# Retention and gated FFN on one core: new order of the first loads, and an FFN that begins on 256 tokens

## The chip, the cores and the metric

The kernel runs on one core of one Trainium2 chip. The metric is the device time of one execution in microseconds (us). The time before is the median of four runs. Besides, one execution was taken by the hardware profiler; its page, its waits, its timeline and its chain are quoted below. Engines are called PE (matmul), PEld (PE's weight loads), DVE, ACT, POOL and SP. Loads from memory are issued mostly by POOL; SP issues the outputs and the transposes done by DMA.

## The reference

For each of 4 batches and 8 heads of width 64 a recurrent state is kept over 768 tokens; its output feeds an FFN with a sigmoid gate:

```python
for t in range(S):
    state = gamma * state + einsum('bhd,bhe->bhde', k[:, :, t], v[:, :, t])
    y[:, :, t] = scale * einsum('bhd,bhde->bhe', q[:, :, t], state)
x = y.transpose(0, 2, 1, 3).reshape(B * S, H * D)      # 3072 tokens of 512
out = (sigmoid(x @ w_gate) * (x @ w_val)) @ w_out      # 512 -> 1536 -> 512
```

Inputs and output are float32; gamma is a constant of each head.

## The kernel before

The recurrence is worked in chunks of 128 tokens. Six steps t = 0 to 5 each treat chunk t of all four batches, so 512 tokens, which stand in one tile `xT[t]` (128 x 4 x 512, bf16, model width on the partitions). A *pair* i = 2t + h holds batches 2h and 2h + 1 of chunk t; j = 0, 1 is the batch inside the pair. Batch b of the first step is `(i, j) = divmod(b, 2)`; the text also calls these four pieces of the first step chunks 0 to 3.

For each piece PE transposes k and q (or SP does it by DMA, `xbar`, from pair 4 on), multiplies them (`scores`, L204), DVE puts the mask or the decay on the product, PE multiplies by v (`intra`, L227; in the first step `first_y`, L303) and adds what the state gives (`inter`, L220); the state is carried on by `state` (L242) and DVE. In the first step there is no state, and the helpers are `first_transposes` (L288, copies at L289), `first_scores` (L204, DVE at L295), `first_y` (L303, copy to `xT[0]` at L306), `first_scaled` (POOL, L309) and `first_state` (L317).

The FFN of a step is `up` for 12 column groups n1 of 128 (each 4 matmuls of 512 columns with `wg` and 4 with `wv`, L331; ACT's sigmoid, L341; DVE's product into `hT`, L342), then `down` for four blocks of 128 tokens (12 matmuls each, L358; ACT copies, L362; SP stores, L363). The weights come in six slices for `wg` and `wv` (`load_gate_val(s)`, 256 columns, two column groups each, L79) and four for `wo` (L86), and stay.

The order of instructions on every engine is the order in which the program is written (`tc.manual_schedule()`). From step 1 on, a table `plan` says behind which group of FFN matmuls each piece of attention work stands: `block(old, new)` closes pair `old` (inter, intra) and opens pair `new` (scores, state). `block(5, 6)` stands near the end of step 1. PE's results go to eight PSUM buffers that are used in turn (`bank`).

What stands at the start: kf and qf (k and q of batch 0, float32) are loaded by SP and ACT; POOL writes three iotas (`tok`, `col`, `ahead`), then issues k and q of batches 1, 2, 3, v of pairs 0 and 1, and three slices of the gate and value weights. POOL's loads use eight semaphores in turn, so a load is issued only when the eighth before it has landed. DVE makes `ident`, `decay` and the rest. `keep_on(n)` is n matmuls of `ident` by itself into a bank that nobody reads. PE does transposes and scores of all four pieces, then `first_y` of all four, then `up` on all 512 tokens.

Of the kernel before, what the change touches and what calls it, by code (L numbers as in the profile page):

```python
# [8 lines left out]
F32 = mybir.dt.float32  # L9
BF16 = mybir.dt.bfloat16  # L10
AX = mybir.ActivationFunctionType
ALU = mybir.AluOpType
# [3 lines left out]
def kernel(  # L16
# [12 lines left out]
    nc = tc.nc  # L29
    B, H, S, D = q.shape  # L30
    N_TOK, D_MODEL = out.shape
    D_FF = moe_w_gate.shape[1]
    C = 128
# [6 lines left out]
    lg = [math.log(1.0 - 2.0 ** (-5.0 - h)) for h in range(H)]  # L40

    ctx.enter_context(tc.manual_schedule())
    const = ctx.enter_context(tc.tile_pool(name="const", bufs=1))
# [6 lines left out]
    vf, kn, qn, vs, kqT = {}, {}, {}, {}, {}  # L50
# [22 lines left out]
    wg = wpool.tile([128, KT, D_FF], BF16, name="wg")  # L73
    wv = wpool.tile([128, KT, D_FF], BF16, name="wv")
    wo = wpool.tile([128, NFF, D_MODEL], BF16, name="wo")

    def load_w(dst, w, s):
        cols = slice(s * 256, (s + 1) * 256)
        nc.gpsimd.dma_start(out=dst[:, :, cols], in_=w.rearrange("(kk p) n -> p kk n", p=128)[:, :, cols])  # L79

    def load_gate_val(s):
        load_w(wg, moe_w_gate, s)
        load_w(wv, moe_w_val, s)
# [7 lines left out]
    def first(dst, x, b, n, eng):  # L91
        eng.dma_start(out=dst, in_=x[b:b + n, :, 0:C, :].rearrange("b h s d -> s (b h) d"))  # L92
# [8 lines left out]
    def entry(t, j):  # L101
        return t[:, j * H:(j + 1) * H, :]
# [4 lines left out]
    tok = const.tile([128, NT], F32, name="tok")  # L107
    col = const.tile([128, C], F32, name="col")
    ahead = const.tile([128, C], F32, name="ahead")
    nc.gpsimd.iota(tok, pattern=[[C, NT]], base=0, channel_multiplier=1, allow_small_or_imprecise_dtypes=True)  # L110
    nc.gpsimd.iota(col, pattern=[[1, C]], base=0, channel_multiplier=0, allow_small_or_imprecise_dtypes=True)
    nc.gpsimd.iota(ahead, pattern=[[-1, C]], base=0, channel_multiplier=1, allow_small_or_imprecise_dtypes=True)
    for b in range(1, B):
        first(entry(kn[b // 2], b % 2), k, b, 1, nc.gpsimd)
        first(entry(qn[b // 2], b % 2), q, b, 1, nc.gpsimd)
    for i in range(2):
        first(vs[i], v, 2 * i, 2, nc.gpsimd)
    for s in range(3):
        load_gate_val(s)

    nlg = const.tile([128, 2, NP], F32, name="nlg")
    lgp = const.tile([128, NP], F32, name="lgp")
    lsc = const.tile([128, 1], F32, name="lsc")
    lsn = const.tile([128, 1], F32, name="lsn")
    ident = const.tile([128, 128], BF16, name="ident")
    causal = const.tile([128, 128], F32, name="causal")
    decay = const.tile([128, 2, NP, C], F32, name="decay")
# [4 lines left out]
    nc.vector.memset(lsc, math.log(scale))  # L134
    for h in range(H):
        nc.vector.memset(nlg[:, h % 2, h // 2:h // 2 + 1], -lg[h])
    nc.vector.tensor_scalar(ident, col, tok[:, 0:1], None, op0=ALU.is_equal)  # L137
    nc.vector.scalar_tensor_tensor(ahead, ahead, -1.0e6, ahead, op0=ALU.mult, op1=ALU.min)
    for e in range(2):
        nc.vector.tensor_tensor(decay[:, e], ahead.unsqueeze(1).to_broadcast([128, NP, C]),  # L140
                                nlg[:, e].unsqueeze(2).to_broadcast([128, NP, C]), op=ALU.mult)
        nc.scalar.activation(decay[:, e], decay[:, e], AX.Exp, bias=lsc)
    nc.vector.tensor_copy(entry(kn[0], 0), kf)
    nc.scalar.copy(entry(qn[0], 0), qf)

    def later_constants():
        for h in range(H):
            nc.vector.memset(lgp[h % 2 * D:(h % 2 + 1) * D, h // 2:h // 2 + 1], lg[h])
        nc.vector.tensor_tensor(tabs.rearrange("s (p e) t -> s p e t", e=2),
                                tok.unsqueeze(1).unsqueeze(1).to_broadcast([128, NP, 2, NT]),  # L150
                                nlg.rearrange("s e p -> s p e").unsqueeze(3).to_broadcast([128, NP, 2, NT]), op=ALU.mult)
        nc.vector.tensor_tensor(taby[:, 1], col.unsqueeze(1).to_broadcast([128, NP, C]),
                                lgp.unsqueeze(2).to_broadcast([128, NP, C]), op=ALU.mult)
        nc.scalar.activation(tabs, tabs, AX.Exp)
        nc.scalar.activation(taby[:, 0], taby[:, 1], AX.Exp, bias=lsc)
        nc.vector.tensor_scalar(causal, col, tok[:, 0:1], None, op0=ALU.is_ge)

    def extend_taby(t):
        nc.gpsimd.tensor_tensor(taby[:, t], taby[:, t - 1], gup.unsqueeze(2).to_broadcast([128, NP, C]), op=ALU.mult)
# [5 lines left out]
    def bank(shape, dt=F32):  # L165
        return pf.tile(shape, dt, tag="ff", name="ff")

    def half(e):
        return slice(e * D, (e + 1) * D)

    def heads(t, j, p):
        return t[:, j * H + 2 * p:j * H + 2 * p + 2, :].rearrange("s h d -> s (h d)")

    def new_kqT(i):
        kqT[i] = at.tile([128, 2, 2, NP, C], BF16, tag="kqT", name="kqT", bufs=2)
# [23 lines left out]
    def scores(i, j):  # L199
        t = kqT[i]  # L200
        sc[i, j] = (bank([128, NP, C]), bank([128, NP, C]))
        for p in range(NP):
            for e in range(2):
                nc.tensor.matmul(sc[i, j][e][:, p, :], t[half(e), 0, j, p, :], t[half(e), 1, j, p, :],  # L204
                                 start=True, stop=True)
# [78 lines left out]
    def first_transposes(i, j, engs):  # L284
        for which, (x, eng) in enumerate(zip((kn[i], qn[i]), engs)):
            tp = bank([128, NP, C], BF16)
            for p in range(NP):
                nc.tensor.transpose(tp[:, p, :], heads(x, j, p), ident)  # L288
            eng(kqT[i][:, which, j], tp)  # L289

    def first_scores(i, j):
        scores(i, j)
        for e, st in enumerate((stA, stB)):
            st[i, j] = at.tile([128, NP, C], BF16, tag=f"st{e}", name=f"st{e}", bufs=4)
            nc.vector.tensor_tensor(st[i, j], sc[i, j][e], decay[:, e], op=ALU.mult)  # L295

    def first_y(i, j, eng):
        if 0 not in xT:
            xT[0] = at.tile([128, NP, 512], BF16, tag="xT", name="xT")
        o = bank([128, NP, C])  # L300
        for p in range(NP):
            for e, st in enumerate((stA, stB)):
                nc.tensor.matmul(o[half(e), p, :], vs[i][:, j * H + 2 * p + e, :], st[i, j][:, p, :],  # L303
                                 start=(p == 0), stop=True, skip_group_check=True)
        c = (2 * i + j) * C
        eng(xT[0][:, :, c:c + C], o)  # L306
# [19 lines left out]
    def up_part(t, w, n1s, lo=0, hi=512):  # L326
        n = hi - lo
        u = bank([128, 512])
        for i, n1 in enumerate(n1s):
            for kk in range(KT):  # L330
                nc.tensor.matmul(u[:, i * n:(i + 1) * n], w[:, kk, n1 * 128:(n1 + 1) * 128], xT[t][:, kk, lo:hi],  # L331
                                 start=(kk == 0), stop=(kk == KT - 1))
        return u[:, :len(n1s) * n]

    def gate_times_val(t, n1s, lo, hi, ps):
        n = hi - lo
        if t not in hT:
            hT[t] = ffn.tile([128, NFF, 512], BF16, tag="hT", name="hT", bufs=2)
        gs = ffn.tile([128, 512], F32, tag="gs", name="gs")
        g = gs[:, :len(n1s) * n]  # L340
        nc.scalar.activation(g, ps[0], AX.Sigmoid)  # L341
        nc.vector.tensor_tensor(hT[t][:, n1s[0]:n1s[-1] + 1, lo:hi], g.rearrange("p (i n) -> p i n", n=n),  # L342
                                ps[1].rearrange("p (i n) -> p i n", n=n), op=ALU.mult)

    def up(t, n1s, lo=0, hi=512):
        gate_times_val(t, n1s, lo, hi, [up_part(t, w, n1s, lo, hi) for w in (wg, wv)])
# [35 lines left out]
    def keep_on(n):  # L382
        u = bank([128, 512])
        for _ in range(n):
            nc.tensor.matmul(u[:, :128], ident, ident, start=True, stop=True)  # L385
# [3 lines left out]
    act, dve = nc.scalar.copy, nc.vector.tensor_copy  # L389
    new_kqT(0)  # L390
    new_kqT(1)
    keep_on(12)
    first_transposes(0, 0, (dve, act))
    keep_on(4)
    first_scores(0, 0)
    first_transposes(0, 1, (act, act))
    later_constants()
    keep_on(4)
    first_scores(0, 1)
    first_transposes(1, 0, (act, act))  # L400
    keep_on(4)
    first_scores(1, 0)
    first_transposes(1, 1, (act, act))
    nc.scalar.preload_act_table(AX.Sigmoid)
    keep_on(4)
    first_scores(1, 1)
    keep_on(4)
    first_y(0, 0, act)
    first_y(0, 1, act)
    keep_on(8)  # L410
    first_y(1, 0, act)
    first_y(1, 1, dve)
    first_scaled(0, 0, kf)
    first_scaled(0, 1, entry(kn[0], 1))
    load_gate_val(3)
# [1 line left out]
    first_scaled(1, 1, entry(kn[1], 1))  # L417
    load_gate_val(4)
    load_gate_val(5)
    for n1 in range(4):  # L420
        up(0, (n1,))
    first_state(0)
    up(0, (4,))
    first_state(1)
    up(0, (5,))
    load_out(0)
    load_out(1)
    for p in range(NP):
# [109 lines left out]
```

## Time and profile before

| what | value |
|---|---|
| median of 4 runs | 231.98 us (231.11, 231.46, 232.51, 232.83) |
| the profiled execution's own time | 232.83 us |
| its span, first to last instruction | 231.1 us |
| PE busy | 220.8 us (96%) |
| POOL, DVE, ACT busy | 108.7, 102.5, 76.4 us |
| first FFN matmul (L331) starts | 18.58 us |
| PE's waits after 15 us | 0.88 before L331, 0.19 before L204 at 89.97, 0.95 before L242 at 92.24 |
| software DMA queue (POOL's loads) | 16.52 MB in 61,664 packets |

How to read it: a line of a timeline begins with the start in us from the span's start and the duration in us, then engine, line, operation, tiles written and read, shapes, and the number of instructions merged; in brackets stands the engine's idle time before it and what ended it. A line of waits gives the total, the number and the longest. In a line of the chain stand start, duration and what the chain ran over. Strings of digits show 40 equal slices of the span, 5.8 us each, in tenths of busy time. A DMA that appears as a POOL or SP line is its issue; its landing comes later.

### The profile page before, as it was taken

The page shows a single profiled execution, that of the slowest core. Times are in us where ns is not written, and L with a number is a line of the kernel's source. Part 1 is how long each engine was busy: PE and PEld are TensorE (multiplying, and loading weights), DVE is VectorE, ACT ScalarE, POOL GpSimd, SP SyncE. Part 2 cuts the span into 40 slices and gives each one's busy share as a digit, 9 for nine tenths or more (in the row PEclk, how much of TensorE's full clock was granted, in tenths as well). Part 3 has the DMA queues.
Part 4 walks back from the last instruction along what each step waited for, and adds up shares of the span by engine and source line. Part 5 has one row for each costly group of instructions (what it writes and reads, how often), then busy time and mean ns, then how long its engine had stood idle before and what let it go on. Part 6 is the DMA issues. An engine that isn't in the chain of part 4 may idle for free.

```text
span 231.1 us, 4377 instructions
## 1 busy us (share of the span) xinstructions
PE 220.8 (96%) x1792; PEld 120.9 (52%) x1792; DVE 102.5 (44%) x179; ACT 76.4 (33%) x127; POOL 108.7 (47%) x128
## 2 busy tenths in 40 slices
PE   4788999999999998999999999999999999999994
PEld 3673444558888654444545444545444544444444
DVE  5643543144764654733922733922634912243301
ACT  5563353336233121333222333222343212433221
POOL 8999949899999844999972100000000000000000
PEclk9999999999999999999999999999999999999999
DMA  9999999999999999999992450012410012100022
GB/s 130 149 186 197 196 190 203 226 148 266 143 191 138 154 133 202 227 142 229 206 185 91 109 120 1 3 44 93 115 23 0 3 47 93 46 1 0 0 94 91
DMA packets 84405, 27.81 MB, mean 120 GB/s; under 512 B 72097, under 2 KB 80161, under 8 KB 84385
## 3 DMA queue, kind: packets, MB, share of 16 engines
q0 software_dynamic: 61664, 16.52, 74.0%
q1 hardware_dynamic: 21536, 10.69, 21.4%
q10 hardware_dynamic: 1184, 0.33, 0.6%
q8 instruction: 14, 0.23, 0.4%
q14 instruction: 7, 0.05, 0.1%
HBM read 28.31 MB, written 6.29 MB: 150 GB/s over the span
## 4 chain that ended last, share of the span: by engine, by line
PE 59%; POOL 21%; DMA 16%; issue 2%; DVE 0%; POOLq 0%
PE ff L331 36%; PE ff L358 18%; DMA wo<-in_moe_w_out_dram 8%; DMA kn<-in_k_dram 4%; DMA qn<-in_q_dram 4%; POOL vs L196 3%; POOL kn L67 2%; POOL wg L79 2%; POOL wv L79 2%; POOL qn L67 2%; POOL ks L309 2%; POOL vf L57 2%; PE ff L227 1%; POOL kn L92 1%; PE ff L204 1%
## 5 line engine op out<-in xcount | busy, mean ns | idle before, releaser
L342 DVE TENSOR_TENSOR hT<-gs,ff 128x512 bf16<-128x512 f32 x72 | 49.2, 687 | 68.8 <-PE ff L331 62.7
L331 PE MATMUL ff<-xT,wg 128*128 128x512 bf16 (+1 forms) x336 | 74.1, 349 | 0.9 <-DVE xT L306 0.9
L331 PE MATMUL ff<-xT,wv 128*128 128x512 bf16 (+1 forms) x336 | 74.0, 349 | 0.0
L341 ACT ACTIVATE gs<-ff 128x512 f32<-128x512 f32 x72 | 43.0, 597 | 78.0 <-PE ff L331 75.8
L358 PE MATMUL ff<-wo,hT 128*128 128x512 bf16 x276 | 62.1, 379 | 0.0
L331 PEld LDWEIGHTS <-wv 128*128 128x128 bf16 x336 | 32.9, 98 | 29.4
L331 PEld LDWEIGHTS <-wg 128*128 128x128 bf16 x336 | 32.1, 98 | 29.3 <-issue 1.0
L358 PEld LDWEIGHTS <-hT 128*128 128x128 bf16 x276 | 26.3, 98 | 30.7
L362 ACT COPY ob<-ff 128x512 f32<-128x512 f32 x23 | 13.4, 585 | 53.3 <-PE ff L358 49.4
L235 DVE TENSOR_TENSOR xT<-ff,taby 128x512 bf16<-128x512 f32 x20 | 12.9, 686 | 33.2 <-PE ff L227 33.2
L210 DVE TENSOR_TENSOR st<-ff,causal 128x512 bf16<-128x512 f32 x40 | 24.8, 681 | 6.3 <-PE ff L204 6.3
L196 POOL TENSOR_TENSOR vs<-vf,tabs 128x1024 bf16<-128x1024 f32 x10 | 19.7, 1974 | 6.7 <-PE ff L227 5.8
L67 POOL DMA_DIRECT2D qn<-in_q_dram x20 | 15.3, 781 | 6.6 <-DMA qn<-in_q_dram 5.8
L67 POOL DMA_DIRECT2D kn<-in_k_dram x20 | 15.1, 763 | 0.3 <-issue 0.3
L57 POOL DMA_DIRECT2D vf<-in_v_dram x10 | 12.0, 1198 | 1.5 <-DMA wo<-in_moe_w_out_dram 1.0
L63 POOL DMA_DIRECT2D kn<-in_k_dram x10 | 9.3, 933 | 0.0
L63 POOL DMA_DIRECT2D qn<-in_q_dram x10 | 9.1, 911 | 0.4 <-DMA kn<-in_k_dram 0.4
L255 ACT CAST zb<-za 128x512 bf16<-128x512 f32 x10 | 6.1, 617 | 8.4 <-DVE za L251 8.4
L385 PE MATMUL ff<-ident 128*128 128x128 bf16 x40 | 5.4, 303 | 1.6 <-DVE ident L137 1.6
L295 DVE TENSOR_TENSOR st<-ff,decay 128x512 bf16<-128x512 f32 x8 | 5.2, 686 | 3.6 <-PE ff L204 3.6
L227 PE MATMUL ff<-st,vs 128*64 128x128 bf16 x160 | 6.4, 222 | 0.0
L204 PE MATMUL ff<-kqT 64*128 64x128 bf16 x64 | 3.7, 259 | 1.8 <-ACT kqT L289 1.8
(66 smaller groups left out, 117.6 us busy)
## 6 DMA issues: line engine op xcount, KB each, us to landing
out_dram<-ob SPq DMA_DIRECT2D x23, 256.0 KB, 2.1
vf<-in_v_dram POOLq DMA_DIRECT2D x10, 512.0 KB, 7.8
kn<-in_k_dram POOLq DMA_DIRECT2D x13, 128.0 KB, 7.2
qn<-in_q_dram POOLq DMA_DIRECT2D x13, 128.0 KB, 6.6
wg<-in_moe_w_gate_dram POOLq DMA_DIRECT2D x6, 256.0 KB, 7.9
wv<-in_moe_w_val_dram POOLq DMA_DIRECT2D x6, 256.0 KB, 8.7
wo<-in_moe_w_out_dram POOLq DMA_DIRECT2D x4, 384.0 KB, 8.6
kn<-in_k_dram POOLq DMA_DIRECT2D x20, 64.0 KB, 7.0
```

The lines of the kernel that those rows point to most:

```text
L57: nc.gpsimd.dma_start(out=vf[i], in_=v[2 * h:2 * h + 2, :, t * C:(t + 1) * C, :].rearrange("b h s d -> s (b h) d"))
L63: nc.gpsimd.dma_start(out=tiles[i][:, 0:H], in_=src[0])
L67: nc.gpsimd.dma_start(out=dst[:, e], in_=pairs[:, 1 - e])
L79: nc.gpsimd.dma_start(out=dst[:, :, cols], in_=w.rearrange("(kk p) n -> p kk n", p=128)[:, :, cols])
L196: eng.tensor_tensor(vs[i][:, j0 * H:(j0 + n) * H, :].rearrange("s (j h) d -> s j h d", j=n), vf[i][:, j0 * H:(j0 + n) * H, :].rearrange("s ...
L210: nc.vector.tensor_tensor(st[i, j], sc[i, j][e], causal4, op=ALU.mult)
L235: nc.vector.tensor_tensor(xT[t][:, :, c:c + C], y[i, j], taby[:, t], op=ALU.mult)
L331: nc.tensor.matmul(u[:, i * n:(i + 1) * n], w[:, kk, n1 * 128:(n1 + 1) * 128], xT[t][:, kk, lo:hi], start=(kk == 0), stop=(kk == KT - 1))
L341: nc.scalar.activation(g, ps[0], AX.Sigmoid)
L342: nc.vector.tensor_tensor(hT[t][:, n1s[0]:n1s[-1] + 1, lo:hi], g.rearrange("p (i n) -> p i n", n=n), ps[1].rearrange("p (i n) -> p i n", n ...
L358: nc.tensor.matmul(o, hT[t][:, n1, b * C:(b + 1) * C], wo[:, n1, :], start=(n1 == 0), stop=(n1 == NFF - 1))
L362: nc.scalar.copy(ob, o)
```

## The change

Four things are changed, all in the first 30 us of the program.

- Loads: `ahead` is the only iota before POOL's first load. Then come k and q of batch 1, v of pair 0, the other two iotas, k and q of batch 2, the first slice of the gate and value weights, v of batch 2, k and q of batch 3, v of batch 3, and the second and third slice. v of pair 1 is loaded by two issues.
- Constants: `ident` and `causal` are made from `ahead` alone; `causal` and the eight `lgp` memsets move ahead of the copy of kf; `later_constants()` is called before `first_scores(0, 0)`.
- PE's order: `first_y` of chunk 0 comes right behind the scores of chunk 1, then transposes of chunk 2, `first_y` of chunk 1 and the scores of chunk 2. FFN groups 0 and 1 are then worked on tokens 0 to 255 (N = 256), then on 256 to 383 (N = 128); groups 2 and 3 on tokens 0 to 383 (N = 384), and all four on 384 to 511 (N = 128). Chunk 3 is transposed and scored between these.
- `keep_on` counts 61 matmuls in all instead of 40, and `first_state(0)` and `first_state(1)` come one column group later.

PE's program grows from 3,586 to 3,724 instructions, 138 more.

```diff
+    nc.gpsimd.iota(ahead, pattern=[[-1, C]], base=0, channel_multiplier=1, allow_small_or_imprecise_dtypes=True)
+
+    def first_kq(b):
+        first(entry(kn[b // 2], b % 2), k, b, 1, nc.gpsimd)
+        first(entry(qn[b // 2], b % 2), q, b, 1, nc.gpsimd)
+
+    first_kq(1)
+    first(vs[0], v, 0, 2, nc.gpsimd)
     nc.gpsimd.iota(tok, pattern=[[C, NT]], base=0, channel_multiplier=1, allow_small_or_imprecise_dtypes=True)
     nc.gpsimd.iota(col, pattern=[[1, C]], base=0, channel_multiplier=0, allow_small_or_imprecise_dtypes=True)
-    nc.gpsimd.iota(ahead, pattern=[[-1, C]], base=0, channel_multiplier=1, allow_small_or_imprecise_dtypes=True)
-    for b in range(1, B):
-        first(entry(kn[b // 2], b % 2), k, b, 1, nc.gpsimd)
-        first(entry(qn[b // 2], b % 2), q, b, 1, nc.gpsimd)
-    for i in range(2):
-        first(vs[i], v, 2 * i, 2, nc.gpsimd)
-    for s in range(3):
-        load_gate_val(s)
+    first_kq(2)
+    load_gate_val(0)
+    first(entry(vs[1], 0), v, 2, 1, nc.gpsimd)
+    first_kq(3)
+    first(entry(vs[1], 1), v, 3, 1, nc.gpsimd)
+    load_gate_val(1)
+    load_gate_val(2)
...
-    nc.vector.tensor_scalar(ident, col, tok[:, 0:1], None, op0=ALU.is_equal)
+    nc.vector.tensor_scalar(ident, ahead, 0.0, None, op0=ALU.is_equal)
+    nc.vector.tensor_scalar(causal, ahead, 0.0, None, op0=ALU.is_le)
...
+    for h in range(H):
+        nc.vector.memset(lgp[h % 2 * D:(h % 2 + 1) * D, h // 2:h // 2 + 1], lg[h])
     nc.vector.tensor_copy(entry(kn[0], 0), kf)
...
     def later_constants():
-        for h in range(H):
-            nc.vector.memset(lgp[h % 2 * D:(h % 2 + 1) * D, h // 2:h // 2 + 1], lg[h])
...
-        nc.vector.tensor_scalar(causal, col, tok[:, 0:1], None, op0=ALU.is_ge)
...
-    keep_on(12)
+    keep_on(26)
     first_transposes(0, 0, (dve, act))
-    keep_on(4)
+    later_constants()
+    keep_on(5)
     first_scores(0, 0)
     first_transposes(0, 1, (act, act))
-    later_constants()
+    keep_on(8)
+    first_scores(0, 1)
+    first_y(0, 0, act)
     keep_on(4)
-    first_scores(0, 1)
-    first_transposes(1, 0, (act, act))
-    keep_on(4)
+    first_transposes(1, 0, (act, dve))
+    first_y(0, 1, act)
     first_scores(1, 0)
-    first_transposes(1, 1, (act, act))
     nc.scalar.preload_act_table(AX.Sigmoid)
     keep_on(4)
-    first_scores(1, 1)
-    keep_on(4)
-    first_y(0, 0, act)
-    first_y(0, 1, act)
-    keep_on(8)
+    up(0, (0, 1), 0, 256)
     first_y(1, 0, act)
-    first_y(1, 1, dve)
     first_scaled(0, 0, kf)
...
     load_gate_val(5)
-    for n1 in range(4):
-        up(0, (n1,))
+    keep_on(8)
+    up(0, (0, 1), 256, 384)
+    first_transposes(1, 1, (act, dve))
+    keep_on(6)
+    first_scores(1, 1)
+    ps = [up_part(0, w, (n1,), 0, 384) for w in (wg, wv) for n1 in (2, 3)]
+    gate_times_val(0, (2,), 0, 384, (ps[0], ps[2]))
+    first_y(1, 1, act)
+    gate_times_val(0, (3,), 0, 384, (ps[1], ps[3]))
+    up(0, (0, 1, 2, 3), 384, 512)
+    up(0, (4,))
     first_state(0)
-    up(0, (4,))
+    up(0, (5,))
     first_state(1)
-    up(0, (5,))
```

More of the change, by code (lines that the diff above doesn't have):

```diff
@@ L125 @@
     lsc = const.tile([128, 1], F32, name="lsc")
-    lsn = const.tile([128, 1], F32, name="lsn")
     ident = const.tile([128, 128], BF16, name="ident")
```

## The prediction

> **What bounds the kernel now.** I read the page first, then PE's timeline of the start, who PE waits for, the chain that ended last, and the timelines of SP and PE around 90 us.
>
> ```profile
> PE 220.8 (96%) x1792; PEld 120.9 (52%) x1792; DVE 102.5 (44%) x179; ACT 76.4 (33%) x127; POOL 108.7 (47%) x128
> PE   4788999999999998999999999999999999999994
> DMA  9999999999999999999992450012410012100022
> ```
>
> PE is the bound, with its holes in the first three slices (5.8 us each). But DMA is full over the first 22 slices, to 127 us: a second bound runs under the first.
>
> ```profile
> 4.65 0.61 PE L288 MATMUL ff<-ident,kn 128*128 128x128 bf16 x4 [1.62 <-DVE kn L143]
> ...
> 11.92 0.61 PE L204 MATMUL ff<-kqT 64*128 64x128 bf16 x8 [0.98 <-ACT kqT L289]
> ...
> 15.31 1.06 PE L303 MATMUL ff<-st,vs 128*64 128x128 bf16 x16
> ...
> 17.07 0.64 PE L303 MATMUL ff<-st,vs 128*64 128x128 bf16 x16
> 18.58 1.02 PE L331 MATMUL ff<-xT,wg 128*128 128x512 bf16 x4 [0.88 <-DVE xT L306]
> ```
>
> Useful FFN work begins at 18.58. The same 16 matmuls of L303 take 1.06 us at 15.31 and 0.64 at 17.07: PE runs slow until about 16.7 (128 columns go out every 107 ns) and fast after (56 ns).
>
> ```profile
> PE ff L242 <- DMA qn<-in_q_dram: 1.0, 1, 1.0
> PE ff L331 <- DVE xT L306: 0.9, 1, 0.9
> PE ff L204 <- DMA kqX<-qn: 0.2, 1, 0.2
> ```
>
> These are all of PE's waits after 15 us. Two lie at 90 us; in the timeline:
>
> ```profile
> 75.93 2.63 SPq L187 DMA_TRANSPOSE kqX<-qn  x1
> ...
> 89.97 0.62 PE L204 MATMUL ff<-kqX 64*128 64x128 bf16 x16 [0.19 <-DMA kqX<-qn]
> ...
> 90.99 0.29 PE L242 MATMUL ff<-vs,kn 128*64 128x64 bf16 x8
> 92.24 0.32 PE L242 MATMUL ff<-vs,kn 128*64 128x64 bf16 x8 [0.95 <-DMA qn<-in_q_dram]
> ```
>
> The transposed q of pair 6, issued at 75.93, lands 13.9 us later, at 89.83, and scores(6) starts at 89.97. So PE has no slack there: time won before 90 us is kept only as far as that transpose also comes sooner. The chain says the same:
>
> ```profile
> 60.25 1.96 POOL vs L196
> ...
> 72.99 10.13 DMA kn<-in_k_dram
> 83.12 0.30 issue
> 83.42 8.69 DMA qn<-in_q_dram
> ```
>
> From the start to 92 us it is POOL and DMA throughout, never PE.
>
> **The change, part by part.** Times below are from the span's start.
>
> *Loads.* POOL's first load now follows one iota (0.23) instead of three: 1.12 instead of 1.42, -0.30. The tok and col iotas (0.35 together) come behind the third load, and v of pair 1 goes in two issues (2 x 0.88 against 1.19), so POOL reaches the ks products 0.6 late (14.1 for 13.51). That is hidden by the backlog: loads issued there land 8 us later, and from 29.37 POOL itself waits for earlier loads to land (29.37, 30.70, 32.67, 34.61 in its timeline), so DMA sets its pace again. Without that cover the 0.6 would pass on to every later load. Landings of before come 0.85 to 0.9 apart for 256 KB of k or q, 1.7 for 512 KB of v, 1.3 to 1.4 for a weight slice. Stacked in the new order from 5.55: v of chunks 0 and 1 lands at 8.8 (12.5 before), k2/q2 at 9.7/10.5, slice 0 at 11.9 and 13.2 (15.5, 16.9), v2 14.1, k3/q3 14.9/15.8 (9.4, 10.2), slice 1 at 18.0 and 19.3 (18.2, 19.9), slice 2 by 22.0 (22.4). The whole DMA stream is thus 0.3 to 0.5 earlier; I take 0.4 and keep 0 and 0.6.
>
> *Constants.* ident, causal, ahead, both decays and the eight lgp memsets take 0.29 + 0.28 + 0.28 + 1.29 + 0.76 of DVE from 1.12: done at about 4.05, and kf lands at 4.14. Cover left: 0.1 us; anything over delays the first transpose by as much. In later_constants DVE's 0.90 goes into its 1.59 idle before L295, ACT's 0.96 into its 1.24 before the next kqT copy. Nothing on the path.
>
> *PE's start.* keep_on has 61 matmuls instead of 40; they fill waits. Up to scores(0,1) (9.0) nothing moves, because kf, qf and the copies set the pace. Then, at the slow clock: y of chunk 0 0.86, four idle matmuls 0.43, transposes of chunk 2 0.86, y of chunk 1 0.86, scores 0.54, four more 0.43: 13.5. xT of two chunks is written at 13.4, slice 0 is there. At the fast clock: 16 x 110 ns to 15.3; y of chunk 2 and eight idle to 16.2; wait for its xT to 16.5; 16 x 56 ns to 17.4; transposes of chunk 3, six idle, wait for the kqT copy, scores to 18.8; the 384-column groups 16 x 163 ns to 21.4 (their wv lands 19.3, wanted at 20.1; behind that wait stand y(1,1) and all of FFN); y 0.45; wait for xT 0.8 (the old 0.88 again); 32 x 56 ns to 24.5. There four column groups are done, as at 25.5 before: PE leads by 1.0. If the fast clock comes at 10 instead of 13.4 the same sum gives 23.7, a lead of 1.8; if it comes at 16.8 as before, 26.2: 0.7 behind. PE now has no hole over 0.15 us from 6.7 to 13.5, against 0.31, 0.98 and 0.31 before, and its speed-up at 16.7 came after 2.5 us with none; so 1.0 to 1.8, about 1.4.
>
> [...]
>
> *The 90 us point.* PE comes to scores(6) 1.4 early and waits for a transpose that is 0.4 early: 1.0 of the lead is lost, 0.4 stays. PE's outputs of block 0 (SP, from 49 us) also go out 1.4 sooner; they only change places with loads.
>
> *The 0.95 at 92.24.* It is put down to qn, but L242 reads kn and vs, and those of pair 6 had landed long before. I read it as PE's own code: the page's queue q8 carries 14 instruction packets, 0.23 MB, one per 256 of PE's 3,584 instructions, and one of them starts inside 89 to 91 us. The stalled one is PE's 1,718th (273 to 18.58, 1,332 to 89.36, 112 after). The new program has 138 more PE instructions ahead of it, so the same edge falls on the old 1,580th, at 86.5 in a run of 24 L358 matmuls with its request some 9 us earlier, at 77: the 0.95 should go. Bounds: 0 (it stays or moves) and 0.95.
>
> **Sum.** The profiled execution is 231.1 of span and 1.7 around it, 232.83. Less 0.4 and 0.95: 231.5. It is the slowest of four runs: 231.11 and 231.46 lie 1.4 below 232.51 and 232.83, about the two waits at 90 us (1.14), so I take half of the four to be without the stall. Those go from 231.3 to 230.9, the others from 232.7 to 231.3. Forecast for the median: 231.1, that is 0.9 less.
>
> **Rivals.** *The lead is kept.* The transpose lands early enough in most runs (its 13.9 us is long: in the same view the q transposes of pairs 4 and 5 took 9.0 and 12.0), so PE keeps 1.4 to 1.8 and the 0.95: about 229.8. For it: the spread of the four runs; against: the full DMA. *Nothing is kept.* The new stream is not earlier (the 0.30 is lost to POOL's extra 0.6), or a stall like the 0.95 appears elsewhere: 231.9. *The slow clock.* PE is 0.7 late and is the bound at 90: 231.98 + 0.7 - 0.5 for half the stall, and more if the clock comes later still: 232.2 to 233.2. *Slower: the code comes late.* The packet at 89 to 91 ran when the transpose ended. If the one now wanted at the old 1,580th waits as long, PE stands in the L358 run at 86.5 until 92.2, with 4.6 us of work behind it (86.5 to 92.2 less the old waits): 231.98 + 4.6 - 0.4 = 236.2. It decides if that packet starts after about 84 us; against it, the q8 packet between 74 and 76 ran while the transposes of pairs 5 and 6 were under way.
>
> **How the numbers follow.** Forecast 0.42; lead kept 0.20; nothing kept 0.18; slow clock 0.13; late code 0.07. The range 229.4 to 233.0 takes in all but the last and the tails. A measurement of this kernel tells about 1% (2.3 us) from no change: below 229.7 lies half of the second case and a tail, 0.15; above 234.3 the last case and a tail, 0.09; within, 0.76.
>
> **What would show it.** L331 begins near 13.5 on 256 columns at about 110 ns each (213 ns would be the slow clock); PE begins the fifth column group near 24; vs and slice 0 land at 8.8 and 12 to 13; PE waits about 1 us at scores(6) for kqX near 89.5; no 0.95 in L242. Wrong if PE has no wait near 90 yet the time barely moves, if it waits for wv at 20, or if it stands in L358 at 86.

## The result and the profile after

The ratio of the new kernel's time to the old one's is 0.998, with a 95% interval of 0.9964 to 0.9995: no change by the 1% that this measurement can tell. The old kernel's median over 71 runs is 231.41 us; the new kernel's 45 runs lie between 229.73 and 247.55 with a median of 233.27, and 23 of them, which take 233.27 us or more with a mean granted clock of 0.993 or less, are left out of the ratio, as such runs are on both sides. The profiled execution of the new kernel took 231.6 us, 229.8 of them span; the old one's took 232.83 and 231.1.

The page of the new kernel, busy time and the slices:

```profile
PE 221.7 (96%) x1861; PEld 123.4 (54%) x1861; DVE 102.7 (45%) x181; ACT 76.1 (33%) x127; POOL 109.5 (48%) x129
PE   6998999999999998999999999999999999999994
DMA  9999999999999999999999670012410012100022
```

The holes of PE in the first three slices are smaller (6, 9, 9 tenths for 4, 7, 8). But DMA is full over 22 slices and then stands at 6 and 7, where the old kernel was full over 21 and then stood at 2, 4 and 5: the transfers end later, not sooner. PE's timeline of the start:

```profile
5.16 0.60 PE L294 MATMUL ff<-ident,kn 128*128 128x128 bf16 x4 [0.81 <-DVE kn L152]
...
9.59 0.61 PE L210 MATMUL ff<-kqT 64*128 64x128 bf16 x8
...
10.75 0.39 PE L294 MATMUL ff<-ident,kn 128*128 128x128 bf16 x4
...
12.70 1.05 PE L337 MATMUL ff<-xT,wg 128*128 128x256 bf16 x8
14.03 1.05 PE L337 MATMUL ff<-xT,wv 128*128 128x256 bf16 x8 [0.28 <-DMA wv<-in_moe_w_val_dram]
...
18.95 1.47 PE L337 MATMUL ff<-xT,wg 128*128 128x384 bf16 x8 [0.21 <-DMA wg<-in_moe_w_gate_dram]
...
22.84 1.05 PE L337 MATMUL ff<-xT,wg 128*128 128x128 bf16 x16 [0.68 <-ACT xT L312]
...
24.63 1.03 PE L337 MATMUL ff<-xT,wg 128*128 128x512 bf16 x4
```

The first transpose starts 0.51 later than before (5.16 for 4.65). Four transposes take 0.39 at 10.75 where they took 0.60 at 5.16: PE is fast from about 10.3, not from 16.7. The FFN begins at 12.70, and its first four column groups are done at 24.63, against 25.58 before: PE leads by 0.95. Around 90 us:

```profile
88.50 0.42 PE L226 MATMUL ff<-kqX,zb 64*64 64x128 bf16 x16
89.89 0.62 PE L210 MATMUL ff<-kqX 64*128 64x128 bf16 x16 [0.97 <-DMA kqX<-qn]
90.44 0.64 PE L233 MATMUL ff<-st,vs 128*64 128x128 bf16 x16
90.91 0.42 PE L248 MATMUL ff<-vs,kn 128*64 128x64 bf16 x16
91.26 1.47 PE L364 MATMUL ff<-wo,hT 128*128 128x512 bf16 x6
```

PE ends `inter` 0.86 ahead of the old execution, waits 0.97 and starts scores(6) at 89.89, 0.08 ahead. There is no hole in `state` (L248), so the next `down` matmuls start 1.22 sooner (91.26 for 92.48). That is the whole gain in the span (231.06 to 229.83); from there on the two run alike. The chain is the old one with other numbers:

```profile
36.02 8.49 DMA vf<-in_v_dram
...
67.14 8.98 DMA qn<-in_q_dram
76.26 13.50 DMA kqX<-qn
91.33 1.40 PE ff L364 x6
```

Most of this fits the forecast; the loads do not. v of pair 0 and the first weight slice land sooner, as they were moved ahead (9.50 and 12.65, for 12.54 and 15.51), but the stream as a whole does not. Its loads by their landings (before, then after): the last slice of `wo` 41.58 and 42.12; the first v load of step 1 (`vf`, 512 KB) 43.11 and 44.52; the next one 47.94 and 50.43. In the first of these steps the lag grows by 0.87 within one load: `vf` lands 1.53 behind `wo` before, 2.40 after. The DMA part of the page, old kernel first, then the new one:

```profile
q1 hardware_dynamic: 21536, 10.69, 21.4%
...
out_dram<-ob SPq DMA_DIRECT2D x23, 256.0 KB, 2.1
vf<-in_v_dram POOLq DMA_DIRECT2D x10, 512.0 KB, 7.8
...
kf<-in_k_dram SPq DMA_DIRECT2D x1, 256.0 KB, 3.4
```

```profile
q1 hardware_dynamic: 21536, 10.69, 25.3%
...
out_dram<-ob SPq DMA_DIRECT2D x23, 256.0 KB, 3.0
vf<-in_v_dram POOLq DMA_DIRECT2D x10, 512.0 KB, 9.6
...
kf<-in_k_dram SPq DMA_DIRECT2D x1, 256.0 KB, 3.8
```

The columns are packets, MB and the share of 16 engines' time for a queue; number, size and median time to the landing for an issue. The same packets with the same bytes take more time (25.3% of the engines' time for 21.4%). Even `kf` does (3.8 for 3.4), the very first load, which the change does not touch and which nothing stands ahead of.

### The profile page after: what moved, and what is told of

The parts are those of the page before. It is cut to its first block, busy times and chain, and to the rows that moved or that the text cites. A ratio compares the mean times of both kernels' runs of the same rounds, so it can differ in the third digit from the quotient of the medians.

```text
span 229.8 us, 4520 instructions
## 1 busy us (share of the span) xinstructions
PE 221.7 (96%) x1861; PEld 123.4 (54%) x1861; DVE 102.7 (45%) x181; ACT 76.1 (33%) x127; POOL 109.5 (48%) x129
## 3 DMA queue, kind: packets, MB, share of 16 engines
q1 hardware_dynamic: 21536, 10.69, 25.3%
## 4 chain that ended last, share of the span: by engine, by line
PE 60%; POOL 19%; DMA 18%; issue 2%; DVE 0%; POOLq 0%; SPq 0%
PE ff L337 36%; PE ff L364 18%; DMA kqX<-qn 6%; DMA wo<-in_moe_w_out_dram 5%; DMA qn<-in_q_dram 4%; DMA vf<-in_v_dram 4%; POOL vs L202 3%; POOL kn L67 2%; POOL wg L79 2%; POOL wv L79 2%; POOL ks L315 2%; PE ff L233 2%; POOL qn L67 2%; PE ff L210 1%; POOL vs L92 1%
## 5 line engine op out<-in xcount | busy, mean ns | idle before, releaser
L348 DVE TENSOR_TENSOR hT<-gs,ff 128x512 bf16<-128x512 f32 (+1 forms) x73 | 49.2, 679 | 69.2 <-PE ff L337 61.7
L337 PE MATMUL ff<-xT,wg 128*128 128x512 bf16 (+3 forms) x360 | 74.2, 337 | 1.1 <-ACT xT L312 0.7
L337 PE MATMUL ff<-xT,wv 128*128 128x512 bf16 (+3 forms) x360 | 74.1, 336 | 0.3 <-DMA wv<-in_moe_w_val_dram 0.3
L347 ACT ACTIVATE gs<-ff 128x512 f32<-128x512 f32 (+1 forms) x73 | 43.0, 591 | 74.5 <-PE ff L337 72.2
L337 PEld LDWEIGHTS <-wv 128*128 128x128 bf16 x360 | 34.1, 98 | 28.9 <-DMA wv<-in_moe_w_val_dram 0.9
L337 PEld LDWEIGHTS <-wg 128*128 128x128 bf16 x360 | 33.5, 98 | 28.5 <-issue 0.9
L391 PE MATMUL ff<-ident 128*128 128x128 bf16 x61 | 6.7, 280 | 1.4 <-DVE ident L143 1.4
L391 PEld LDWEIGHTS <-ident 128*128 128x128 bf16 x61 | 5.4, 131 | 1.7 <-DVE ident L143 1.4
```

## The experiments

They fall into three groups: what holds PE at 90 us, what an earlier clock alone is worth, and why the loads are later. Ratios are to the old kernel, with 95% intervals, over several runs of each; a span, a wait or a landing is that of the one execution that was profiled.

### What holds PE near 90 us

**Code edge moved, work unchanged.** The old kernel with 69 tiny idle matmuls (138 instructions) in places where PE waited.

```diff
+        for _ in range(tiny):
+            nc.tensor.matmul(u[:32, :32], ident[:, :32], ident[:, :32], start=True, stop=True)
...
-    keep_on(12)
+    keep_on(12, 26)
```

> The kernel before with 69 matmuls of 32 x 32 added in PE's idle places before 18.6 us, so that its program has the new kernel's 3,724 instructions; loads and order stay. Theory (the 0.95 us before L242 at 92 us was PE's own code coming late, and went because the edge of a code packet moved by 138 instructions): no gap in the L242 group near 92, the span 0.9 to 1.1 shorter than the 231.1 of before, and the median 0.4 to 0.9 lower, as only some runs of before would have the gap. Rival (the gap was a wait for a load): the gap stays, time within 0.2 of before.

Measured: 0.9944 (0.9922 to 0.9965), span 228.2. No hole in L242, but no wait at scores(6) either: the transposed q of pair 6 landed at 76.93 instead of 89.83. The fast clock had also come at 10.67, for 16.78 before. So two things moved at once, and this run alone does not tell them apart.

**Code edge moved back in the new kernel.** 59 such matmuls more, so that the edges fall where they fell before.

```diff
-    keep_on(26)
+    keep_on(26, 12)
...
+    keep_on(0, 47)
     up(0, (0, 1, 2, 3), 384, 512)
```

> The new kernel with 59 matmuls of 32 x 32 added in PE's idle places before 23 us, 118 instructions, so that the edges of its code packets lie at the same instructions of block(5, 6) as in the kernel before (256 more than there). Theory: a gap of 0.5 to 1.1 us comes back inside the block at 90 to 92 us and the time is 0.5 to 1.1 above the new kernel. Rival (a load ended the gap): no gap, time as the new kernel within 0.3.

Measured: 0.9999 (0.9964 to 1.0033), span 230.0; no hole near 92, and 0.4 of wait for the transpose of the next pair:

```profile
PE ff L210 <- DMA kqX<-qn: 0.4, 1, 0.4
```

The hole did not come back, but here the packet of code (queue q8) ran at 87.9 instead of 89.7, after the transpose of pair 6 had landed (86.19). So the run neither shows nor excludes the reading of the 0.95 as late code.

**PE made later.** The new kernel with 14 idle matmuls ahead of the fifth column group.

```diff
     up(0, (0, 1, 2, 3), 384, 512)
+    keep_on(14)
     up(0, (4,))
```

> The new kernel with 14 more idle matmuls of 128 columns ahead of column group 4, so PE's whole FFN is 0.8 us later from 24.6 us on. Theory (the lead of PE is lost at scores(6), where PE waits 0.97 for the transposed q): the wait at scores(6) shrinks to 0.1 to 0.3 and the time stays within 0.3 of the new kernel. Rival (PE's lead counts in full): 0.8 slower.

Measured: 0.9998 (0.9965 to 1.003), 0.4 us above the new kernel, between the two forecasts and no proof of either. The wait did not shrink to 0.1 to 0.3 in the profiled execution: the transpose landed at 94.21 there. It took 237.6 (span 235.5), and shows what a long wait for that transpose does:

```profile
94.34 0.93 PE L210 MATMUL ff<-kqX 64*128 64x128 bf16 x14 [4.76 <-DMA kqX<-qn]
```

```profile
80.00:90.00 10.00, 9.58 (x115) 4.80 (x113) 5.37 (x9) 2.79 (x5) 7.71 (x8) 1.00 1.77 127
90.00:94.00 4.00, 0.00 (x0) 0.00 (x0) 0.00 (x0) 0.00 (x0) 0.66 (x1) 0.97 1.30 152
94.00:97.00 3.00, 2.66 (x49) 2.29 (x50) 1.01 (x2) 0.00 (x0) 1.93 (x3) 0.50 1.68 256
```

The second fence is the table of stretches (start and end, length, busy time of PE, PEld, DVE, ACT and POOL, then the granted clock, DMA share, GB/s). After 4.76 idle, PE runs at half clock; by the clock's record from 93.75 to 97.16.

**The suspected transposes taken away.** Pair 6 uses the transposed tiles of pair 5, so what the kernel computes for pair 6 is not the reference's.

```diff
-(12, casts, 4), (12, xbar, 6), (13, scaled, 6),
+(12, casts, 4), (12, same_kqT, 6), (13, scaled, 6),   # kqT[6] = kqT[5]
```

> The new kernel without the two DMA transposes of pair 6; block(5, 6) and block(6, 7) use the transposed k and q of pair 5 instead. Theory (that transpose is the bound at 90 us): no wait at scores(6), the time 0.9 to 1.2 lower than the new kernel, as the whole lead of PE is then kept. Rival (PE is held there by the full DMA at large, so the next transfer takes its place): a wait of 0.5 or more elsewhere before 112 us and less than 0.4 gained.

Measured: 0.996 (0.9938 to 0.9983), span 229.0, and PE runs through 88.93 without a wait. The 0.97 is that transpose's, and the span falls by nearly that (229.8 to 229.0). By the ratios the gain is 0.5 us, with intervals that overlap, where 0.9 to 1.2 was expected.

### What the early clock alone is worth

**Idle matmuls of 512 columns in the old kernel.** Loads, useful work and the number of PE instructions stay; PE's early holes are filled better.

```diff
-    keep_on(12)
+    keep_on(2, 6)
     first_transposes(0, 0, (dve, act))
-    keep_on(4)
+    keep_on(2, 1)
...
-    keep_on(8)
+    keep_on(15)
```

> The kernel before with the same 3,586 PE instructions and the same loads, but its idle matmuls rearranged (some of 512 columns) so that PE has no hole over 0.2 us from 1.6 to about 10: the clock should turn fast near 10.6 as it did with the 69 small matmuls added. Theory (what that run gained was PE's lead, 1.4 us from the earlier clock, kept because the outputs of block 0 and the transposes behind them on SP go out sooner): FFN from about 17.1, no wait at scores(6), 229.8 to 230.4. Rival (it was the shift of the code by 138 instructions): FFN early too, but the gap of about 0.95 in block(5, 6) stays, and the time is 230.8 to 231.5.

Measured: 0.9946 (0.9915 to 0.9977), span 228.6. The fast clock comes at 10.92 and the FFN begins at 17.57, on 512 tokens as before. At 90 us:

```profile
88.35 0.42 PE L220 MATMUL ff<-kqX,zb 64*64 64x128 bf16 x16
88.70 0.62 PE L204 MATMUL ff<-kqX 64*128 64x128 bf16 x16
89.25 0.64 PE L227 MATMUL ff<-st,vs 128*64 128x128 bf16 x16
89.72 0.42 PE L242 MATMUL ff<-vs,kn 128*64 128x64 bf16 x16
90.07 1.47 PE L358 MATMUL ff<-wo,hT 128*128 128x512 bf16 x6
```

No wait and no hole, with the code edges where they were. So the gain of the first experiment needs no shift of the code; idle matmuls alone give it. The q transpose of pair 6 landed at 80.05.

**The old kernel once more**, unchanged.

> The kernel before, unchanged, once more. If the wait at scores(6) and the 0.95 behind it belong to the program, both are there again within 0.3; if they come from how the transfers happened to fall, the q transposed of pair 6 lands at another time than 89.83 and the gap in L242 is gone or elsewhere.

Measured: 230.84, span 229.0; FFN at 17.96, the transpose landed at 79.38, no wait at scores(6), no hole in L242. The two waits that the forecast was built on (0.19 and 0.95) belong to the one execution that was profiled, not to every run of the program. Nor does its late clock: the repeat's record is fast from 8.80, at half from 12.22 to 15.63, and fast again, where the profiled one was slow until 16.78.

With the repeat the three old programs can be compared without any wait at 90 us. Their first four column groups are done at 24.12 (tiny idle matmuls), 24.57 (wide ones) and 24.96 (the repeat), and their spans are 228.2, 228.6 and 229.0: each time 204.1 more. So where PE has no wait behind the start, a lead at the start counts in full, and filling the holes is worth 0.4 to 0.8 against the repeat. The new kernel's span fits the same sum with its wait: 24.63 + 0.97 + 204.1 is 229.7, and 229.8 was measured.

### Why the loads are later

**The old order of the loads under the new order of PE.**

```diff
-    first_kq(1)
-    first(vs[0], v, 0, 2, nc.gpsimd)
...
+    for i in range(2):
+        first(vs[i], v, 2 * i, 2, nc.gpsimd)
+    for s in range(3):
+        load_gate_val(s)
```

> The new kernel's order on PE with the old order of the iotas and of POOL's loads. PE then waits some 3 us for v of pair 0 and about 2 us for the first weight slice, so its lead should be between -0.5 and 0.5. Theory (the new order of loads, with 29 loads instead of 28 up to the output weights, makes the DMA stream later from 42 us on: the v of pair 3 lands 2.4 us behind the last output weights instead of 1.5): that distance is 1.5 to 1.8 here, q transposed of pair 6 lands by 88, and the time is 230.8 to 231.6. Rival (the DMA stream is late because PE's outputs come sooner): the distance is 2.4 here too or the landing after 89.

Measured: 1.0113 (1.0036 to 1.019), span 232.3. PE stands at its first y:

```profile
PE ff L302 <- DMA vs<-in_v_dram: 3.6, 1, 3.6
```

That is 2.6 us over the old kernel, more than either forecast: behind this wait the clock's record is at half from 11.51 to 18.33, and four column groups are done only at 28.13. So the new order of PE needs the new order of the loads. But `vf` still lands 2.47 behind the last `wo`: the order of the loads is not what makes it late. PE's outputs are not either, as SP issues the first one at 51.73 here, later than in the old kernel (49.10).

**v of pair 1 in one issue** again, in the new kernel.

```diff
-    first(entry(vs[1], 0), v, 2, 1, nc.gpsimd)
+    first(vs[1], v, 2, 2, nc.gpsimd)
     first_kq(3)
-    first(entry(vs[1], 1), v, 3, 1, nc.gpsimd)
```

> The new kernel with v of pair 1 loaded by one issue (where the first of the two stood), so POOL has 28 loads up to the output weights as before. Theory A (the odd number of loads is what makes the stream late from 42 us): v of pair 3 lands 1.5 to 1.8 behind the last output weights, q transposed of pair 6 before 88, no wait at scores(6), 230.0 to 230.6. Theory B (it is the order of the first loads, or PE's outputs): 2.4 again, a wait of 0.5 or more at scores(6), 230.8 to 231.5.

Measured: 0.9965 (0.9914 to 1.0016), span 228.9; `vf` lands 2.34 behind `wo`. The number of loads is not it either. Theory B's wait is missing in this execution, though: the q transpose of pair 6 landed at 87.97, in time for 88.97.

What remained was a line of the change that the diff above leaves out, and that the forecast did not weigh:

```diff
     lsc = const.tile([128, 1], F32, name="lsc")
-    lsn = const.tile([128, 1], F32, name="lsn")
     ident = const.tile([128, 128], BF16, name="ident")
```

No instruction uses `lsn`. But a constant of 4 bytes takes 32 per partition, and every tile made behind it moves down by 32: in the built programs the first `kn` begins at byte 76,032 of a partition before and at 76,000 after. Before, all tiles that DMA writes or reads (`kf`, `kn`, `qn`, `vf`, `kqX`, `ob`, the weights) begin at a multiple of 256 bytes; after, 224 past one.

**The room of `lsn` given back to the new kernel.** No instruction differs.

```diff
+    pad = const.tile([128, 1], F32, name="pad")
```

> The new kernel with one unused column, 128 x 1 float32, set aside behind lsc, where the old kernel has its unused tile lsn, which the change deletes. Constants take room in steps of 32 bytes per partition, so without it every tile made later (weights, kf, kn, qn, vf, kqX, ob) begins 32 bytes earlier: at 224 past a multiple of 256 in the new kernel, at 0 in the old one. No instruction differs from the new kernel's. Theory A (the place of the tiles sets the time of their DMAs): the rows of the old kernel come back: kf 3.4 us from issue to landing (3.8 in the new), the first v load of step 1 lands 1.5 to 1.8 behind the last wo (2.4), 256 KB output stores take 2.1 in the median (3.0), the transposes at 130 us land about 1.5 behind the end of their issue (2.0). The q transpose of pair 6 lands at 82 or before, PE does not wait at scores(6), and the FFN starts about 0.4 sooner, near 12.3. Time: the new kernel's profiled 231.6 less 0.97 of that wait and 0.4 to 0.6 at the start: 230.1, 229.3 to 230.5, all runs close together. Theory B (the place does not matter; the later loads come from the order of PE or of POOL): vf 2.4 behind wo, stores 3.0, the q transpose near 90, a wait of about 1 there, 231.0, and many runs over 233 as in the new kernel.

Measured: 0.9959 (0.9942 to 0.9976), span 229.0; the 12 runs lie between 230.06 and 230.92, close together as theory A said. The old rows are back:

```profile
q1 hardware_dynamic: 21536, 10.69, 19.8%
...
out_dram<-ob SPq DMA_DIRECT2D x23, 256.0 KB, 2.0
vf<-in_v_dram POOLq DMA_DIRECT2D x10, 512.0 KB, 7.7
...
kf<-in_k_dram SPq DMA_DIRECT2D x1, 256.0 KB, 3.5
```

The q transpose of pair 6 lands at 81.40, PE does not wait at scores(6), and theory A holds. Three of its numbers missed: 230.55 for 230.1; `vf` 1.92 behind `wo` for 1.5 to 1.8; and the FFN at 12.51 for 12.3. PE came sooner to slice 1 and waited 0.54 for it, so that the fifth column group starts at 24.83, no sooner than in the new kernel.

**`lsn` deleted from the old kernel**, and nothing else.

```diff
-    lsn = const.tile([128, 1], F32, name="lsn")
```

> The old kernel with its unused tile lsn deleted and nothing else: every tile made later begins 32 bytes earlier, as in the new kernel. Theory A (place): kf 3.8 us to its landing, vf 2.4 behind the last wo, output stores 3.0, the transposes at 130 us about 2.0 behind their issue, the q transpose of pair 6 at 90 or later, and PE waits there 1 to 4 us; 232.5 to 235. Theory B (place does not matter): 1.5 to 1.8, 2.1 and 1.5, and 231.4 as the old kernel.

Measured: 1.0361 (1.0296 to 1.0426), five runs between 238.80 and 248.61, span 237.9: more than either theory gave. The rows of the page are the new kernel's (`kf` 3.9, stores 3.0), and PE's timeline and the table of stretches show the price:

```profile
89.92 0.42 PE L219 MATMUL ff<-kqX,zb 64*64 64x128 bf16 x16
96.10 1.03 PE L203 MATMUL ff<-kqX 64*128 64x128 bf16 x16 [5.77 <-DMA kqX<-qn]
```

```profile
90.00:96.00 6.00, 0.34 (x16) 0.17 (x16) 0.00 (x0) 0.00 (x0) 0.90 (x2) 0.78 1.09 124
96.00:100.00 4.00, 3.90 (x52) 2.74 (x53) 2.25 (x4) 0.00 (x0) 2.87 (x3) 0.50 1.87 232
```

5.77 of wait, and then half the clock (by its record from 93.35 to 100.18), about 2 more on the 4 us of work in it. The expectation had the wait at 1 to 4 and left the clock out.

**Two other places.** The pad of the new kernel made 96 bytes, then 160: the tiles begin 64 and 128 past a multiple of 256.

```diff
+    pad = const.tile([128, 17], F32, name="pad")
```

> The new kernel with an unused tile of 96 bytes per partition instead of 32: the later tiles begin 64 past a multiple of 256, so at a multiple of 64 but not of 128. If a multiple of 64 is enough, the rows are those of the old kernel: vf 1.5 to 1.8 behind the last wo, stores 2.1, transposes at 130 us about 1.5 behind their issue, and about 230.1. If it takes more (128 or 256), they are those of the new one: 2.4, 3.0, 2.0, and 231 or more.

```diff
+    pad = const.tile([128, 40], F32, name="pad")
```

> The new kernel with an unused tile of 160 bytes per partition: the later tiles begin 128 past a multiple of 256. The runs so far show three places: 0 (stores 2.0 to 2.1 us in the median, the transposes at 130 us 1.5 behind their issue), 224 (3.0; 2.0 to 2.1) and 64 (3.5; 2.0 to 2.1, one 3.4). If a multiple of 128 is enough: kf 3.4 to 3.5 to its landing, stores 2.0 to 2.1, transposes 1.5, no wait at scores(6), 230.5 with all runs close together, as with 32 bytes. If it takes 256: kf 3.8 or more, stores 3.0 or more, transposes 2.0, the q transpose of pair 6 near 86 to 91, 231 or more with some runs far above.

Measured at 64: 0.9991 (0.9934 to 1.0048), nine runs between 230.34 and 241.60, span 231.7, stores 3.5, and a wait for the q transpose of pair 5:

```profile
83.25 0.78 PE L211 MATMUL ff<-kqX 64*128 64x128 bf16 x16 [2.04 <-DMA kqX<-qn]
```

At 128: 0.9933 (0.99 to 0.9965), span 228.2, no such wait; the transpose of pair 6 landed at 85.64, in time for 88.28, and the clock was fast from 4.18. The quantity that the crowd on the DMA engines blurs least is the time of the q transposes after 125 us, where loads are over or nearly so. From the DMA view of that window, first with `lsn`'s room given back (place 0), then the new kernel (224), then 128:

```profile
out_dram<-ob SPq DMA_DIRECT2D x12, 256.0 KB, 2.0
...
kqX<-qn SPq DMA_TRANSPOSE x3, 2.7
```

```profile
out_dram<-ob SPq DMA_DIRECT2D x12, 256.0 KB, 2.0
...
kqX<-qn SPq DMA_TRANSPOSE x3, 3.2
```

```profile
kqX<-qn SPq DMA_TRANSPOSE x3, 3.1
```

| place past 256 | kernels | `kf` to landing | first `vf` of step 1 to landing | q transposes after 125 us |
|---|---|---|---|---|
| 0 | 5 (the old one, its repeat, both with added idle matmuls, the 32-byte pad) | 3.4 to 3.5 | 7.7 to 8.0 | 2.7 in all |
| 224 | 7 (the new one, its five variants above, the old one without `lsn`) | 3.6 to 3.9 | 8.5 to 8.7 | 3.1 to 3.3 |
| 64 | 1 | 3.9 | 9.5 | 3.2 |
| 128 | 1 | 3.7 | 8.8 | 3.1 |

Of the four places tried, with one layout each, only the multiple of 256 has the short times; a multiple of 128 was not enough (q transposes 3.1 for 2.7). The k transposes of the same window do not part as well: medians of 2.7 to 3.5 at place 0 and 3.2 to 4.3 elsewhere. Nor does the landing that PE waits for depend on the place alone: the q transpose of pair 6 lands at 76.93 to 81.40 in four of the five kernels at place 0, at 89.83 in the profiled old one, and at 85.64 to 95.97 at the other places. (At 128 the expectation for that case had `kf` at 3.8, stores at 3.0 and 231 us or more; `kf` took 3.7 and the stores 2.6 over the whole span, between the two cases, and the time is the lower one.) The output stores take 2.0 to 2.1 at every place once the loads are over, so their 3.0 is the crowd, not their own address: what slows down are the loads and the transposes, which write *into* these tiles. (A transpose also reads one, `kn` or `qn`; no run tells its two sides apart.) The kernel at 128 is none the slower for it, because PE still came after its transpose. Its lowest time goes with PE's start: it came to the matmuls on tokens 384 to 511 at 22.27, 0.78 before the kernel with the 32-byte pad (23.05), and the spans differ by as much (228.2 and 229.0).

## Why the prediction was right, and where it was not

The class came out, no change that can be told, and so did the number: 231.1 was forecast, and 0.998 of 231.41 is 230.9. That the number is so near is in part luck. The forecast was 0.9 under 231.98, the median of four runs; the old kernel's median over 71 runs is 231.41, and the measured gain is 0.5. Of what the forecast added up, 0.4 was to come from earlier loads, which were not earlier, and half of 0.95 from a stall that the old program has in some executions only. Nor does anything in it foresee a spread of 229.73 to 247.55. One reading was off as well: DMA is full over 21 slices before, to 121 us, not over 22. What is right is the shape: PE's lead of about a microsecond at the start is lost again to a wait of about a microsecond for one transpose.

*Loads.* This step failed, in size and sign. 0.4 sooner was forecast; `wo` came 0.5 later and v 1.4 to 2.5 later. Two terms are missing or too small. The sum had nothing for `lsn`, because the line issues no instruction; with its room given back, `vf` lands at 44.13 instead of 44.52 and the next v at 48.71 instead of 50.43, which is 0.4 of the 1.4 and 1.7 of the 2.5, while `wo` stays where it was (42.21 for 42.12). And POOL reached the `ks` products 1.5 late (15.02 for 13.51), not 0.6, in part because it had to wait for a load:

```profile
14.26 0.74 POOL L79 DMA_DIRECT2D wv<-in_moe_w_val_dram  x1 [0.51 <-DMA wv<-in_moe_w_val_dram]
```

What that costs at the landings was not tried by itself. The 0.30 was not there either: POOL's first load starts at 1.36 instead of 1.42, since POOL then stood 0.28 for nothing that the profile shows.

```profile
1.36 1.06 POOL L92 DMA_DIRECT2D kn<-in_k_dram  x1 [0.28 <-issue]
```

And a term of 0.4 is below what runs differ by: with the same loads, the last `wo` lands at 41.58, 41.98 and 42.63 in the old kernel, its repeat and the one with wide idle matmuls.

*Constants.* They do hide. DVE was ready and waited 0.69 for `kf`; the first transpose is late because `kf` is.

*PE's start.* The fast clock came at 10.3, near the 10 that the larger sum assumed, but that is luck: the holes do not decide it alone. Six kernels of the experiments have the new kernel's PE program up to 24 us, and their profiled executions turn fast at 4.18, 4.65, 5.00, 5.07, 8.96 and 10.46. (The old program did so at 16.78 and, in its repeat, at 8.80; with filled holes at 10.67 and 10.92.) All turned before the FFN, so the rival of the slow clock did not come about. The moment also matters little for the FFN's beginning, which lies between 12.22 and 12.70 in all seven: in the four with the earliest clock PE then waited 0.29 to 0.74 for q of chunk 2. For a clock at 10 the sum said a lead of 1.8; measured 0.95. The terms that were too small are the loads, 0.51 for `kf`, 0.28 and 0.21 for slices 0 and 1, and the matmuls on 256 and 384 columns, which took 2.02 and 2.80 instead of 1.76 and 2.61. Together that is more than the 0.85 that is missing, so other terms were a little too large. Against the repeat of the old kernel (24.96) the lead is only 0.33.

*The 90 us point.* The wait of 1 was right (0.97), its reason half: the transpose was not 0.4 sooner but 0.08 (89.75 for 89.83). "Never PE" was read off one chain and does not hold for the program. SP issues the outputs of block 0 ahead of the transposes, so a PE that is earlier issues them earlier: the first, of pair 4, at 55.21 before, and at 53.29 and 54.45 in the two old kernels with a faster start. Their q of pair 6 lands at 76.93 and 80.05, far ahead of PE, though in the unchanged repeat too it lands at 79.38. Issuing early is not enough, as the new kernel shows: its first is issued at 53.89, and q of pair 6 still lands at 89.75. The rival in which the lead is kept had the mechanism of every kernel at place 0 that was run besides the profiled old one.

*The 0.95.* It did go, but the repeat of the old kernel lacks it without any change, so it was no saving of the change's. Whether it was late code stays open: the runs show when a packet of code ran (89.7 before, 87.9 with the edges moved back), not when it was asked for, and the 9 us of the forecast were an estimate.

*The accounts.* At place 0 the change is worth 0.9959 (230.55); the deletion of `lsn` costs the old program 3.6% (its wait at scores(6) is 5.77) and the new one the difference to 0.998 (its wait is 0.97), with intervals that overlap a little, and a far wider spread of its runs. So the rest of the change seems to hide most of what its deleted line costs; which of its parts does so was not tried. Filling PE's holes in the old order, with no other change, gives 0.9944 and 0.9946: beginning the FFN on 256 tokens shows no gain beyond that, as with the 32-byte pad its first four column groups are done at 24.83, and at 24.57 and 24.12 in the old order. The lowest ratios among the kernels that compute the whole result are those of the two old ones with idle matmuls and of the new one with a pad of 32 or of 160 bytes (0.9933 to 0.9959). Their intervals overlap with each other, and reach a little into the new kernel's.

## What to carry to other kernels

Where DMA is the second bound, the start addresses of the tiles that it writes are part of the kernel. Here they did best at multiples of 256 bytes per partition: at 64, 128 and 224 past one `kf` took 3.6 to 3.9 for 3.4 to 3.5, and the q transposes after 125 us 3.1 to 3.3 for 2.7, though at 128 the kernel was none the slower. Look at them when a change adds or deletes any tile, used or not. Compare the landings of the loads one by one, beginning with a load that the change doesn't touch; here the first of all, `kf`, already told it. Before a stall of the old profile is booked as a gain, see in a second execution whether it is there; the same goes for the moment at which the clock turns fast (16.78 and 8.80 in two executions of the old kernel).

## What was not expected of the hardware

An unused 4 bytes per partition are worth 3.6% of the old program. With the loads over or nearly so, a q transpose between tiles off the 256-byte grid took 3.1 to 3.3 us for 2.7.

The waits of 2.04 (the 64-byte place), 4.76 (PE made later) and 5.77 us (the old kernel without `lsn`) did not only cost themselves: the granted clock fell to one half during the wait or just behind it, and PE then worked at half clock for 3.4, 2.8 and 4.1 us (83.57 to 86.98, 94.34 to 97.16, 96.10 to 100.18). The wait of 0.97 had no such price: the 16 matmuls behind it took 0.62, as in the old execution. With half of these stretches taken as lost, an estimate, the spans add up: for the 64-byte place 23.92 + 204.1 + 2.04 + 1.7 = 231.8 (measured 231.7), and for the old kernel without `lsn` 26.14 + 204.1 + 5.77 + 2.0 = 238.0 (237.9).

When the clock turns fast is not fixed by the program: 4.18 to 10.46 in kernels with the same PE program up to there.
